# A linear-attention block and a gated MLP on one core: the second MLP product by Strassen's seven products, in items of 256 tokens by 1024 hidden columns

## The chip, the cores and the metric

The kernel runs on one core of a Trainium2 chip. The metric is device time in microseconds of one execution, the median of several. Engines are named as the profile names them: PE is the matrix engine (PEld its weight loads), DVE the vector engine, ACT the scalar engine with its function tables, POOL the general engine, SP the queue that issues most DMAs.

## The reference

Eight batches of eight heads, 576 tokens of width 64. Softmax of `q` over the head width, softmax of `k` over the tokens, then a linear attention, and a gated MLP over all 4608 tokens. `moe_w_in` and `moe_w_out` arrive as float64.

```python
q_s = softmax(q, axis=-1)            # per token
k_s = softmax(k, axis=2)             # per feature, over the tokens
kv  = einsum('bhsd,bhse->bhde', k_s, v)
x   = einsum('bhsd,bhde->bhse', q_s, kv)   # -> (4608, 512)
h   = x @ w_in                       # (4608, 512) @ (512, 2048)
sp  = maximum(h, 0) + log1p(exp(-abs(h)))
g   = h * erf(sp)
out = g @ w_out                      # (4608, 2048) @ (2048, 512)
```

## The kernel before, in words

**Precision.** An fp32 operand is written as the sum of two float16 tiles, a high and a low one (`split2`: ACT writes the high part, DVE the rest). A product of two such operands takes three float16 matmuls (high·high, high·low, low·high). A float32 matmul shows in the trace as two records. The first token block uses float32 matmuls in both MLP products, because the weights' split parts do not exist yet at that time.

**Weights.** Each of the eight jobs in `JOBS` is a quarter of `w_in` or `w_out`. A job is loaded as raw 64-bit words in two pieces (`wload`), turned into float32 by three DVE instructions for each piece (`wdecode`, `D` in the order), squared and reduced on ACT for a scale (`wsquares`, `Q`), and, once all eight are there, scaled in common (`wscales`, `Z`) and split (`wsplit`, `S`). For `w_in` the split also makes the sums that Strassen's scheme needs (`wsplit_sums`, `R`): seven operands in place of four. `w_out` is split plainly.

**First product.** It works in items: 384 tokens by 512 hidden columns, 12 blocks times 4 groups, 48 items, numbered n. `mm1(n, k)` (line 881 on) makes the seven Strassen products of an item, each of 12 matmuls of 192 columns into one of three PSUM banks X, Y and Z. The evacuations add them up in `H`: three by ACT, four by DVE. The operands of x, seven again, are made once per block by `finish`. Items 0 to 3 use `mm1_32`.

**Activation.** `softplus` and `erf` (`T`, `G`, line 337 in the trace, since both go through the helper `act`) run on ACT, each behind a load of its function table. `gmul` (`U`, line 984) multiplies on DVE. `ghi` and `glo` (`I`, `O`, lines 997 and 1001) split the result on DVE into two float16 halves, which lie in the memory of `H`.

**Second product.** `mm2(n, tt)` (line 1007 on) is plain: for each of three token tiles, four row blocks of `w_out` times three float16 matmuls of 512 columns (line 1029), accumulated over the four items of a block. Items 0 to 3 use float32 (line 1020). The last item's sum is scaled and moved out by one DVE instruction per token tile (line 1045), and SP issues the store.

**Attention.** `attention(b)` is a generator. Each `A` in the order, and `pace` later on, takes its next piece. It takes the two halves of the heads through column maxima of k, exponentials, the kv product and norms of q, then transposes q and makes x.

**What sets the order.** `ORDER` is a list by hand for items 0 to 3 and the weights. After it the loop over n emits, for each n, `U(n-1)`, the pieces of `m(n)`, of the split of n-1 and of `M(n-2)` interleaved, attention by `pace` against `SHARES`, and `T(n)`, `G(n)`. The framework then orders each engine's instructions by priority (order of emission) and by when its planner takes the operands to be there, so an engine's queue is not simply the order written. Each engine works its queue in order. A tile pool's `bufs` says how many copies of a tile exist, and a writer waits until the readers of the copy it takes are done.

```python
for n in range(4, N + 2):
    m0, m1, m2 = n < N, n - 1 < N, n - 2 < N
    if m1: tok(f"U{n - 1}")
    for i in range(4):
        if m0: tok(f"m{n}.{i}")
        if 4 < n <= N and i < 2: tok(f"{'IO'[i]}{n - 1}")
        ...
        if m2 and i < 3:
            tok(f"M{n - 2}.{i}")
            pace(n + (i + 1) / NTT)
```

## Time and profile before

| | us |
|---|---|
| median of three runs (lowest to highest) | 866.37 (865.97 to 866.99) |
| span of the profiled execution | 865.1 |
| PE busy, share of the span | 823.4, 95% |
| DVE busy | 642.5, 74% |
| ACT busy | 505.9, 58% |
| POOL busy | 18.2, 2% |

The page gives one time for the profiled execution, its span from the first to the last instruction. The median of the runs is 1.3 us above it, which is what lies around the span. Busy time is a union: where two instructions of an engine overlap, the time counts once. A "mean ns of one" is an instruction's own duration, and neighbours overlap by part of it. Matmuls overlap most: how often they follow each other is read from the start of one group to the start of the next.

### The profile page before, as it was taken

The numbers are of one execution on the slowest core, as the hardware profiler recorded it, in microseconds if no ns is written. First come the engines' busy times: TensorE is split into PE (matmuls) and PEld (weight loads), VectorE is DVE, ScalarE is ACT, GpSimd is POOL, SyncE is SP. The second block draws the span as 40 slices with busy tenths as digits, with TensorE's granted clock in tenths as the row PEclk, the third lists the DMA queues.
The fourth block names the chain that finished last, engine by engine and source line by source line (L and its number), as shares of the span: only waits on it lengthen the run. The fifth ranks groups of instructions, "written<-read, shape, count | busy, mean of one in ns | idle before, by whom it ended". The sixth has DMA issues, their size and how long they took to land.

```text
span 865.1 us, 15558 instructions
## 1 busy us (share of the span) xinstructions
PE 823.4 (95%) x6556; PEld 570.3 (66%) x6556; DVE 642.5 (74%) x923; ACT 505.9 (58%) x646; POOL 18.2 (2%) x37
## 2 busy tenths in 40 slices
PE   3999996889999999999999999999999999999997
PEld 2655555557766677767776677776776677677672
DVE  6999799899887778858866778867865656653543
ACT  2697677576584567466655467466655456453532
POOL 2101100000000000000000000000000000000000
PEclk9999998889999999999999999999999999999999
DMA  9976730041223202311141212311010000000100
GB/s 270 402 166 184 187 86 1 1 104 26 61 50 80 65 23 50 80 38 25 33 103 32 56 30 50 80 38 25 20 43 2 24 15 1 37 2 1 37 2 37
DMA packets 117381, 55.53 MB, mean 64 GB/s; under 512 B 106560, under 2 KB 108608, under 8 KB 117312
## 3 DMA queue, kind: packets, MB, share of 16 engines
q1 hardware_dynamic: 115136, 46.15, 20.3%
q0 software_dynamic: 2176, 8.39, 2.7%
q8 instruction: 51, 0.84, 0.4%
q14 instruction: 18, 0.15, 0.0%
HBM read 45.09 MB, written 9.44 MB: 63 GB/s over the span
## 4 chain that ended last, share of the span: by engine, by line
PE 73%; DVE 13%; ACT 6%; SPq 3%; DMA 2%; issue 2%; POOL 0%; ACTq 0%; DVEq 0%
PE o L1029 33%; PE pX L905 17%; PE pZ L905 8%; PE pY L905 4%; PE kv L535 3%; ACT L337 2%; ACT G L337 2%; SPq L402 2%; DVE wt L290 2%; PE o L1020 2%; DVE G L984 2%; PE x L625 2%; PE qT L610 1%; DVE H L1001 1%; DMA q<-in_q_dram 1%
## 5 line engine op out<-in xcount | busy, mean ns | idle before, releaser
L1029 PE MATMUL o<-wt,H 128*128 128x512 f16 x1584 | 366.9, 380 | 3.6 <-DVE H L997 3.1
L905 PEld LDWEIGHTS <-wt 128*128 128x128 f16 x3696 | 312.4, 99 | 37.5 <-issue 15.2
L1029 PEld LDWEIGHTS <-H 128*128 128x128 f16 x1584 | 152.4, 98 | 159.0 <-DVE H L997 4.1
L905 PE MATMUL pX<-x,wt 128*128 128x192 f16 x2112 | 208.0, 249 | 9.8 <-ACT H L924 5.7
L337 ACT ACT_TABLE_LOAD x105 | 134.7, 1283 | 7.9 <-DVE H L930 5.7
L984 DVE SCALAR_TENSOR_TENSOR G<-G,small,H 128x1536 f32<-128x1536 f32 x44 | 80.0, 1817 | 65.9 <-ACT G L337 65.8
L905 PE MATMUL pZ<-x,wt 128*128 128x192 f16 x1056 | 103.4, 247 | 0.0
L932 ACT COPY H<-pX 128x384 f32<-128x384 f32 x44 | 20.9, 476 | 139.7 <-PE pX L905 134.7
L337 ACT ACTIVATE G<-H,U 128x768 f32<-128x768 f32 (+1 forms) x60 | 72.8, 1231 | 22.1 <-DVE H L930 21.5
L1001 DVE TENSOR_TENSOR H<-G,H 128x1536 f16<-128x1536 f32 x44 | 77.3, 1756 | 1.1
L337 ACT ACTIVATE G<-G 128x1536 f32<-128x1536 f32 x48 | 71.2, 1484 | 0.5
L905 PE MATMUL pY<-x,wt 128*128 128x192 f16 x528 | 51.1, 246 | 0.5 <-DVE H L917 0.5
L436 ACT ACTIVATE x<-x 128x384 f32<-128x384 f32 (+1 forms) x52 | 17.6, 386 | 56.4 <-PE x L625 54.0
L917 DVE COPY H<-pY 128x384 f32<-128x384 f32 x44 | 24.4, 555 | 30.1 <-PE pY L905 30.1
L997 DVE CAST H<-G 128x1536 f16<-128x1536 f32 x44 | 42.0, 955 | 0.7
L290 DVE SCALAR_TENSOR_TENSOR x<-x,x 128x768 f16<-128x768 f32 (+1 forms) x44 | 37.2, 850 | 5.7 <-ACT x L289 5.6
L289 ACT ACTIVATE x<-x 128x768 f16<-128x768 f32 (+1 forms) x44 | 33.1, 762 | 12.2 <-DVE x L381 12.1
L1045 DVE TENSOR_SCALAR ob<-o,V 128x512 f32<-128x512 f32 x29 | 21.7, 749 | 23.9 <-PE o L1029 23.7
L930 DVE TENSOR_TENSOR H<-pZ,H 128x384 f32<-128x384 f32 x44 | 24.2, 551 | 19.3 <-PE pZ L905 19.3
L919 DVE TENSOR_TENSOR H<-pX,H 128x384 f32<-128x384 f32 x44 | 24.4, 555 | 15.3 <-PE pX L905 14.9
L535 PE MATMUL kv<-vbuf,k 128*64 128x65 f32 x480 | 22.0, 237 | 7.6 <-ACT k L337 5.2
L535 PEld LDWEIGHTS kv<-vbuf,k 128*64 128x64 f32 x480 | 18.7, 149 | 14.5 <-ACT k L337 6.4
(162 smaller groups left out, 823.1 us busy)
## 6 DMA issues: line engine op xcount, KB each, us to landing
out_dram<-ob SPq DMA_DIRECT2D x32, 256.0 KB, 2.2
vbuf<-in_v_dram SPq DMA_DIRECT2D x60, 128.0 KB, 3.0
q<-in_q_dram SPq DMA_DIRECT2D x56, 128.0 KB, 3.0
k<-in_k_dram SPq DMA_DIRECT2D x56, 128.0 KB, 3.3
wt<-in_moe_w_out_dram POOLq DMA_DIRECT2D x5, 1024.0 KB, 6.5
wt<-in_moe_w_in_dram SPq DMA_DIRECT2D x4, 1024.0 KB, 10.7
raw<-in_moe_w_in_dram SPq DMA_DIRECT2D x2, 1024.0 KB, 14.3
wt<-in_moe_w_out_dram SPq DMA_DIRECT2D x2, 1024.0 KB, 16.0
```

Of the source, the lines that this page charges most:

```text
L289: nc.scalar.activation(hi, src, AF.Copy, scale=s)
L290: nc.vector.scalar_tensor_tensor(lo, src, s, hi, op0=ALU.mult, op1=ALU.subtract)
L337: i = nc.scalar.activation(out_, in_, func, **kw)
L535: nc.tensor.matmul(bk[a * D:(a + 1) * D, c * W:(c + 1) * W], kk, vv, start=(t == 0), stop=(t == TM),)
L905: nc.tensor.matmul(o, w[wl][:, c, a * P:(a + 1) * P], x[:, xl, xi, c, :], start=(new and a == 0 and c == 0 and i == 0), stop=(c == 1 and i ...
L917: nc.vector.tensor_copy(C[0, 0], bank2("Y"))
L919: add(C[0, 0], bank2("X"), C[0, 0], op=ALU.add)
L930: add(C[0, 1], bank2("Z"), C[0, 1], op=ALU.add)
L984: nc.vector.scalar_tensor_tensor(flat(s["G"]), flat(s["G"]), GA[:, g:g + 1], flat(s["H"]), op0=ALU.mult, op1=ALU.mult,)
L997: nc.vector.tensor_copy(flat(s["gh"]), flat(s["G"]))
L1001: nc.vector.tensor_tensor(flat(s["gl"]), flat(s["G"]), flat(s["gh"]), op=ALU.subtract)
L1029: nc.tensor.matmul(o, s[gt][:, a, ts_], w[wl][:, a, :], start=(first_ and a == 0 and i == 0), stop=(last_ and a == FG - 1 and i == 2),)
```

## The change

The second product becomes a Strassen product too, and the items change shape: 256 tokens by 1024 hidden columns, 18 blocks times 2 groups, 36 items.

- `mm1` makes seven products of 24 matmuls with 128 columns, in two PSUM banks (X, Y), evacuated in tiles of 128x512: four by ACT, three by DVE.
- `mm2` makes seven products of 12 matmuls with 256 columns. The operands are made from G by `gsums` (four DVE instructions of 512 columns) and `gs` (four splits, three of 1024 columns and one of 512: the high part by ACT, the low part by DVE) into one buffer `GS`. `evacuate` adds up a block's output with seven DVE instructions of 256 columns and one on ACT (two more ACT scalings in blocks that hold tokens of two batches).
- The four `w_out` jobs are split into seven operands like those of `w_in`.
- Blocks 0 and 1 (items 0 to 3) do the second product in float32 (`mm2_32`); only block 0 (items 0 and 1) does the first one in float32 (`mm1_32`).
- The x operands are made in four parts (`finish` "a" to "d") inside the last item of the block before.
- Attention takes one half of the heads after the other, with one buffer for k instead of two (the second half's k and v are loaded after the first half's kv product), and is paced by `DUE`.
- In `ORDER` batch 1's attention stands behind the scales; all weights are decoded ahead of them.
- `H` has two buffers instead of three, `G` one instead of two, `ob` two instead of three.

```diff
-    ("in", 0), ("in", 1), ("out", 0), ("in", 2), ("out", 1), ("in", 3), ("out", 2),
-    ("out", 3),
-]
-CHAIN_FROM, CHAIN_TAIL = 2, 11
+JOBS = [(w, g) for w in ("in", "out") for g in range(4)]
+CHAIN_FROM, CHAIN_TAIL = 1, 6
...
-    m0.0 m0.1 D0.0.1 D0.1.1 D1.0 D1.1 m0.2 m0.3 T0 G0 Q0
-    D2.0 A m1.0 D2.1 m1.1 U0 m1.2 m1.3 T1 G1 Q1 A A D3.0 M0.0 D3.1 M0.1 M0.2 Q2 U1 A A
...
+    D0.0.1 D0.1.1 m0.0 m0.1 D1.0 D1.1 m0.2 m0.3 T0 G0 Q0 Q1
+    D2.0 D2.1 m1.0 m1.1 D3.0 D3.1 U0 m1.2 m1.3 Q2 Q3
+    D4.0 D4.1 D5.0 D5.1 T1 G1 M0.0 M0.1 Q4 Q5 D6.0 D6.1 U1 D7.0 D7.1 Q6 M1.0 Q7 M1.1
+    Z S0 R0 S1 R1 fa fb fc fd m2.0 m2.1 m2.2 m2.3 m2.4 m2.5 m2.6 T2 G2
+    A A S2 R2 A S3 R3 U2 A A A A A A A
+    m3.0 m3.1 fa m3.2 M2.0 m3.3 m3.4 fb fc M2.1 m3.5 fd m3.6 T3 G3 S4 R4 S5 R5
+    U3 M3.0 M3.1 S6 R6 S7 R7
...
+DUE = {2: 7, 3: 11, 4: 17, 5: 21, 6: 25, 7: 29}
+LEAD = 0.5
...
-        if which == "out":
-            split2(stg.pop(jn), whalf(jn, 0), whalf(jn, 1), s)
+        wsplit_n(jn, 0, sg[:, :, :256], 2)
+        wsplit_n(jn, 2, Q[1, 1], 1)
...
+        for o, x, y, op in sums:
+            nc.vector.tensor_tensor(Q[o], Q[x], Q[y], op=op)
...
+            t = at.tile(
+                [P, TM, 4, D], F32, tag=tag, bufs=1 if tag == "k" else 2, name=f"{tag}_{b}_{hf}"
+            )
...
+        if key == "a":
+            x_operands(i, "a", x[:, :, :P])
+            sub((0, 0), (0, 1), (0, 0))
+            sub((0, 1), (1, 1), (0, 1))
+        elif key == "b":
+            x_operands(i, "b", Bk[1, 1])
+            sub((1, 1), (1, 1), (0, 0))
+            sub((1, 0), (1, 0), (1, 1))
+        elif key == "c":
+            x_operands(i, "c", x[:, :, :P])
+        else:
+            x_operands(i, "d", x[:, :, P:])
+            x_next[0] += 1
...
         for hf in range(2):
+            ks = d["k"][hf]
...
+            kv_norm(b, hf, kv_mm(b, hf))
+            if hf == 0:
+                load_kv(b, 1)
+            elif b + 1 < B:
+                load_kv(b + 1, 0)
+            yield 1.5
+            q_norm(rows(qs[hf]), 16, f"q_{name}", b)
...
+    PRODS = [("Y", 1, 1), ("X", 0, 0), ("Y", 6, 3), ("X", 3, 6), ("Y", 4, 2), ("X", 5, 5),
+             ("X", 2, 4)]
...
+        for gi, jn in enumerate(jns):
+            w = [wop(jn, h, wi, 1)[:, 0] for h in range(2)]
+            for a in range(2):
+                o = s[b][:, (2 * gi + a) * P:(2 * gi + a + 1) * P]
+                for c in range(2):
+                    for t, (wl, xl) in enumerate(((0, 0), (0, 1), (1, 0))):
+                        nc.tensor.matmul(
+                            o, w[wl][:, c, a * P:(a + 1) * P], x[:, xl, c, :],
...
+        if k_ in (0, 2, 3, 6):
+            nc.scalar.copy(C[{0: (0, 0), 2: (1, 1), 3: (0, 1), 6: (1, 0)}[k_]], ev)
+        else:
+            o = C[{1: (0, 0), 4: (0, 1), 5: (1, 1)}[k_]]
+            add(o, ev, o, op=ALU.add)
...
-            for a in range(FG):
-                for i, (gt, wl) in enumerate((("gh", 0), ("gh", 1), ("gl", 0))):
-                    nc.tensor.matmul(
-                        o, s[gt][:, a, ts_], w[wl][:, a, :],
...
+    def gsplit(t, src):
+        nc.scalar.copy(t[:, 0], src)
+        nc.vector.tensor_tensor(t[:, 1], src, t[:, 0], op=ALU.subtract)
...
+        for o, x, y, op in ((
+            (S_[0], A[1, 0], A[1, 1], ALU.add), (S_[1], S_[0], A[0, 0], ALU.subtract),
+        ), (
+            (S_[2], A[0, 0], A[1, 0], ALU.subtract), (S_[3], A[0, 1], S_[1], ALU.subtract),
+        ))[e]:
+            nc.vector.tensor_tensor(o, x, y, op=op)
...
+        o = acc[bi][:, half * 256:half * 256 + 256]
...
+                for t, (gl, wl) in enumerate(((0, 0), (0, 1), (1, 0))):
+                    nc.tensor.matmul(
+                        o, g[:, gl, f, :], w[wl][:, a, :],
...
+        if k_ == 1:
+            nc.scalar.activation(ob[1][:, l], acc[0][:, l], AF.Copy, scale=1.0 if mixed else V[0])
+            plus(ob[0][:, l], 0, 1, ob[1][:, l])
+        elif k_ == 4:
+            plus(ob[1][:, l], 1, 1, ob[1][:, l])
+            plus(ob[0][:, r], 1, 0, ob[1][:, l])
+        elif k_ == 6:
+            plus(ob[1][:, r], 2, 0, ob[0][:, r])
+            plus(ob[0][:, r], 2, 1, ob[0][:, r])
+            plus(ob[1][:, l], 2, 0, ob[1][:, l])
+            plus(ob[1][:, l], 3, 0, ob[1][:, l])
...
+    def mm2_32(n, j):
...
+        for f in range(FT):
+            w = STG[JOBS.index(("out", 2 * u + f // 4))]
+            nc.tensor.matmul(
+                o, st[n]["H"][:, f, j * P:(j + 1) * P], w[:, f % 4, :],
...
+    FIN = {1: "fa", 4: "fb fc", 5: "fd"}
+    GSP = {0: "g{}.0", 1: "s{}.0 g{}.1", 2: "s{}.3", 4: "s{}.1", 6: "s{}.2"}
     for n in range(4, N + 2):
-        m0, m1, m2 = n < N, n - 1 < N, n - 2 < N
+        m0, m1, m2 = n < N, 4 <= n - 1 < N, 4 <= n - 2 < N
...
+        for i in range(7):
             if m0:
                 tok(f"m{n}.{i}")
...
+            if m2:
                 tok(f"M{n - 2}.{i}")
+            if m1:
+                for o in GSP.get(i, "").split():
+                    tok(o.format(n - 1))
+            if m0:
+                pace(n + (i + 1) / 7)
```

More of the change, by code (lines that the diff above doesn't have):

```diff
@@ L673, in attention @@
-        q_norm(rows(qs[1]), 16, f"q_{b}_1", b)
-        if j == 1:
+        yield 1.6
+        if tailq:
             q_norm(even["qt"], H, f"qt_{p}", b)
-        yield SHARES[8]
-        for i in ((3 * p + 1, 3 * p + 2) if j else (3 * p, 3 * p + 1)):
-            while not x_free(i):
-                yield 0
-        if j == 1:
+            yield 1.3
+        c0 = 0 if j == 0 else SM
+        blks = [x[0] for x in xcols(b, c0, SM if j == 0 else SM + P)]
+        while not all(x_free(i) for i in blks):
+            yield 0
@@ new lines, in vscale, with quad @@
+    def vscale(tau):
+        bs = batches(tau)
+        if len(bs) == 1:
+            return gscale(bs[0])
+        d = bat[bs[1]]
+        if "Vt" not in d:
+            d["Vt"] = at.tile([P, 1], F32, tag="Vt", bufs=1, name=f"Vt_{bs[1]}")
+            for a, b in enumerate(bs):
+                ps = slice(a * TAIL, (a + 1) * TAIL)
+                nc.vector.tensor_copy(d["Vt"][ps], gscale(b)[ps])
+        return d["Vt"]
+    def quad(t):
+        return t.rearrange("p (g q a) t -> p g q a t", g=2, q=2)
@@ L956, in unit @@
+    def unit(b, u):
+        U = bat[b]["U"][:, u:u + 1]
+        if b < 2 and (b, u) not in udone:
+            udone.add((b, u))
+            nc.vector.tensor_tensor(U, w_u["in"][:, u:u + 1], bat[b]["ux"], op=ALU.mult)
         return U
@@ L1046, in mm2, with evacuate, plus @@
-        if last_:
-            for dst, src in out_dmas(p, bk * NTT + tt, obs[i0, tt]):
-                nc.sync.dma_start(dst, src)
+                        o, g[:, gl, f, :], w[wl][:, a, :],
+                        start=(u == 0 and half == 0 and gi == a == t == 0),
+                        stop=(u == NU - 1 and gi == a == 1 and t == 2), skip_group_check=True,
+                    )
+        if u == NU - 1:
+            evacuate(i, k_)
+    def evacuate(i, k_):
+        V = [vscale(2 * i + j) for j in range(2)]
+        mixed = V[0] is not V[1]
+        if k_ == 0:
+            obs[i] = [at.tile([P, DM], F32, tag="ob", bufs=2, name=f"ob_{i}_{j}")
+                      for j in range(2)]
+        ob = obs[i]
+        l, r = slice(0, 256), slice(256, 512)
+        def plus(o, bi, half, y):
+            src = acc[bi][:, half * 256:half * 256 + 256]
+            if mixed:
+                nc.vector.tensor_tensor(o, src, y, op=ALU.add)
+            else:
+                nc.vector.scalar_tensor_tensor(o, src, V[0], y, op0=ALU.mult, op1=ALU.add)
+        if k_ == 1:
[9 more added lines that the diff above has]
+            plus(ob[1][:, l], 3, 0, ob[1][:, l])
+            for j in range(2):
+                if mixed:
+                    nc.scalar.activation(ob[j], ob[j], AF.Copy, scale=V[j])
+                out_dma(2 * i + j, ob[j])
@@ L1050, in attn_moe_kernel @@
     steps = start()
-    fn = dict(T=softplus, G=erf, U=gmul, I=ghi, O=glo)
+    fn = dict(T=softplus, G=erf, U=gmul)
     emitted_steps = set()
```

737 lines of the change are left out of this document (337 added, 400 removed).

## The prediction

> **What bounds the kernel now.** I read the page's busy shares, the busy time by stretches, then the chain in order of time for the length of a period, and the waits.
>
> ```profile
> PE 823.4 (95%) x6556; PEld 570.3 (66%) x6556; DVE 642.5 (74%) x923; ACT 505.9 (58%) x646; POOL 18.2 (2%) x37
> ```
>
> ```profile
> 0.00:22.00 22.00, 7.65 (x58) 5.87 (x59) 14.51 (x20) 6.03 (x6) 5.13 (x13) 1.00 1.04 273
> ...
> 800.00:865.00 65.00, 58.87 (x419) 36.88 (x416) 28.90 (x30) 25.89 (x25) 0.00 (x0) 1.00 0.07 25
> ```
>
> ```profile
> 22.00:200.00 178.00, 162.37 (x951) 102.48 (x950) 165.37 (x259) 130.52 (x198) 10.53 (x16) 0.94 0.47 137
> 107.00:200.00 93.00, 77.76 (x579) 54.98 (x578) 88.50 (x145) 65.83 (x83) 1.59 (x3) 0.89 0.18 45
> 254.00:450.00 196.00, 194.70 (x1738) 140.05 (x1737) 151.99 (x227) 113.72 (x140) 1.90 (x6) 1.00 0.22 54
> 420.50:435.20 14.70, 14.70 (x157) 11.23 (x156) 14.40 (x21) 10.01 (x13) 0.00 (x0) 1.00 0.29 80
> ```
>
> The columns are stretch, length, then busy PE, PEld, DVE, ACT, POOL, and the granted clock. There are two regimes. From 254 to 450 us PE works 194.70 of 196 us: PE is the bound, with DVE at 78% and ACT at 58%. From 107 to 200 us, where the weights are split, DVE is the bound: 88.50 of 93 us (95%), with PE at 84%. The first 22 us and the last 65 cost PE 14.4 and 6.1 us of idleness.
>
> ```profile
> 450.61 1.58 ACT G L337
> ...
> 646.31 1.58 ACT G L337
> ```
>
> ```profile
> DVE G L984 <- ACT G L337: 65.8, 33, 6.6
> ```
>
> The pattern of the chain repeats after 195.70 us, which is two batches: 12 items. DVE's longest wait is that of `U` for the error function: 65.8 us, 1.5 for each of the 44 items of line 984, 6.6 at most.
>
> **PE's part.** Start to start in the timeline gives what one matmul costs in a stream:
>
> ```profile
> 92.78 2.74 PE L944 MATMUL pZ<-x,wt 128*128 128x384 f32 x8
> 95.36 2.74 PE L944 MATMUL pX<-x,wt 128*128 128x384 f32 x8
> ...
> 104.21 2.74 PE L1020 MATMUL o<-sg,G 128*128 128x512 f32 x6
> 106.79 1.02 PE L622 MATMUL x<-qTs,kvbd 128*128 128x512 f32 x2
> ...
> 127.26 1.15 PE L905 MATMUL pY<-x,wt 128*128 128x192 f16 x12
> 128.25 1.15 PE L905 MATMUL pX<-x,wt 128*128 128x192 f16 x12
> ...
> 228.19 2.75 PE L1029 MATMUL o<-wt,H 128*128 128x512 f16 x12
> 230.78 1.15 PE L905 MATMUL pZ<-x,wt 128*128 128x192 f16 x12
> ```
>
> That is 82.5 ns at 192 columns (0.99/12), 215.8 at 512 (2.59/12), and 322 and 430 for a float32 record of 384 and 512. The line through the first two has 0.4166 ns a column; it gives 55.8 ns at 128 columns and 109.2 at 256, and 216 for a float32 record of 256 (twice the columns).
>
> No row has 128 columns. The nearest below is this one, of 64 columns, each with its own weight load:
>
> ```profile
> 277.63 0.83 PE L625 MATMUL xt<-qTt,kvbd 128*128 128x64 f16 x23
> 278.30 1.24 PE L1029 MATMUL o<-wt,H 128*128 128x512 f16 x5
> ```
>
> It gives 0.67/23 = 29 ns, on the same line (29.2). So weight loads don't hold a 128-column stream; I take 55.8, between 29 and 82.5 as bounds.
>
> An item before: 84 x 82.5 + 36 x 215.8 ns = 6.93 + 7.77 = 14.70 us. After: 168 x 55.8 + 84 x 109.2 = 9.37 + 9.17 = 18.55 us, for 4/3 of the work. Float32 records: before 4 x 16 x 2 = 128 in the first product and 4 x 12 x 2 = 96 in the second; after 2 x 32 x 2 = 128 and 4 x 16 x 2 = 128. Totals: before 44 x 14.70 + 128 x 0.322 + 96 x 0.430 = 729; after 34 x 9.37 + 32 x 9.17 + 128 x 0.216 + 128 x 0.430 = 695. PE is relieved of 34 us. A batch's attention costs PE (195.7 - 12 x 14.70)/2 = 9.65 us, unchanged.
>
> **DVE's part**, which the change loads:
>
> ```profile
> L984 DVE SCALAR_TENSOR_TENSOR G<-G,small,H 128x1536 f32<-128x1536 f32 x44 | 80.0, 1817 | 65.9 <-ACT G L337 65.8
> L1001 DVE TENSOR_TENSOR H<-G,H 128x1536 f16<-128x1536 f32 x44 | 77.3, 1756 | 1.1
> L997 DVE CAST H<-G 128x1536 f16<-128x1536 f32 x44 | 42.0, 955 | 0.7
> L919 DVE TENSOR_TENSOR H<-pX,H 128x384 f32<-128x384 f32 x44 | 24.4, 555 | 15.3 <-PE pX L905 14.9
> L604 DVE TENSOR_TENSOR qTs<-qT,qTs 128x512 f16<-128x512 f32 x24 | 16.5, 686 | 9.1 <-ACT qTs L603 9.1
> L290 DVE SCALAR_TENSOR_TENSOR wt<-wt,small,wt 128x1024 f16<-128x1024 f32 x12 | 15.1, 1280 | 2.3 <-ACT wt L289 2.3
> L315 DVE TENSOR_TENSOR wt<-wt 128x512 f32<-128x512 f32 x16 | 10.9, 684 | 0.0
> L491 DVE TENSOR_TENSOR kmax<-k 128x256 f32<-128x256 f32 x16 | 6.7, 418 | 0.1
> L290 DVE SCALAR_TENSOR_TENSOR wt<-wt,small,wt 128x2048 f16<-128x2048 f32 x2 | 4.7, 2348 | 0.0
> L290 DVE SCALAR_TENSOR_TENSOR wt<-wt,small,wt 128x512 f16<-128x512 f32 x4 | 3.0, 748 | 0.0
> ```
>
> Per item before: four evacuations of 0.555, 1.82, 0.955 and 1.756 = 6.7 us for 1536 columns. After, for 2048: three evacuations of 0.686, `U` 2.35, `gsums` 4 x 0.684, and splits of 3 x 1.22 (between the 512 and the 1536 row) and 0.686: 2.06 + 2.35 + 2.74 + 4.35 = 11.5 us. The cast goes to ACT, but it was DVE's cheapest. To this come, per item, 1.7 us of `evacuate` (seven times 0.48 per two items; 256 columns from the 512 and 1024 rows of line 290) and 2.2 us of `finish` (three 0.748, one 0.48, four 0.418 per two items): 15.4 us. Neighbours overlap by some 0.07 us each; 20 instructions make it 14.0.
>
> Over the kernel: evacuations 70, `U` 85, sums 88, splits 139, `evacuate` 54, `finish` 75 us against 390 before; the weights' splits 8 x 7.3 = 59 against 38; halved attention +4. That is +144, less 0.07 x 240 more instructions: +127, so 769 us of DVE. Attention stays near 27 us a batch: (152 - 12 x 6.25 - 9 x 0.68 - 3 x 5.0)/2 plus the halves.
>
> So in iterations 4 to 28, which carry six batches, PE needs 25 x 18.55 + 58 = 522 us and DVE 25 x 14.0 + 162 = 512. The cover under which DVE's extra work would be free is gone.
>
> **ACT.** Per item four copies of 0.59, `softplus` and `erf`, two table loads, and splits of 3 x 1.06 + 0.59 (`softplus` and `erf` are the 1536-column rows times 4/3, less their fixed part):
>
> ```profile
> L337 ACT ACT_TABLE_LOAD x105 | 134.7, 1283 | 7.9 <-DVE H L930 5.7
> L337 ACT ACTIVATE G<-H,U 128x1536 f32<-128x1536 f32 x28 | 44.1, 1576 | 0.3
> L337 ACT ACTIVATE G<-G 128x1536 f32<-128x1536 f32 x48 | 71.2, 1484 | 0.5
> L337 ACT ACTIVATE k<-k 128x1024 f32<-128x1024 f32 x14 | 14.7, 1056 | 10.6 <-DVE k L648 10.2
> L603 ACT CAST qTs<-qT 128x512 f16<-128x512 f32 x24 | 14.1, 588 | 19.1 <-PE qT L610 19.1
> ```
>
> That is 2.4 + 2.0 + 1.9 + 2.6 + 3.8 = 12.6 us, and some 16 with attention and `finish`, of 20.9: busy, not the bound, though it stands in the loop `erf`, `U`, splits, `M`. Table loads fall from 48 pairs to 36 and rise by one per batch.
>
> **The start.** The scales come at 111.4 us now, with batch 1's attention (some 26 us of DVE) ahead of them:
>
> ```profile
> 111.39 0.18 DVE L250 TENSOR_REDUCE small<-sq 128x8 f32<-128x32 f32 x1
> ```
>
> After, it stands behind them: scales at about 87. Then DVE owes 59 (splits) + 29 (batch 1) + 9 + 4 + 5 = 105, less overlaps 96 us; at the 95% of the stretch from 107 us, 101. Item 4 has its way from 188 us, with the first products of items 4 and 5 done by then in PE's gaps.
>
> **DMA queues.** The second half's k and v wait for the first half's kv product on SP, ahead of q loads and output stores:
>
> ```profile
> k<-in_k_dram SPq DMA_DIRECT2D x56, 128.0 KB, 3.3
> ```
>
> Four issues of about 1 us and 3.3 to land are some 7 us, twice per batch. I take 0: a batch has four items, 84 us. Uncovered, it would be up to 42 us for six batches. The single buffers of `G` and `GS` cost 0 as well: from one `softplus` to the next through `erf`, `U`, sums and two splits it is 6.5 + 7.0 = 13.5 us, under 18.55.
>
> **The sum.** From 188 us PE still has 32 x 9.17 + 30 x 9.37 + 6 x 9.65 = 632 us. The end costs about 9 (6.1 now, plus a longer way through `evacuate`). 188 + 632 + 9 = 829 if PE never waits. But DVE needs 512/25 = 20.5 us per item against PE's 20.87, and it now idles 1.5 us per item at `U`. I keep that wait, since nothing that causes it goes away: 22.0 us, 1.13 more than PE, 28 us over 25 items. Span 857; with 1.3 us around it, **858**. DVE would then be busy 93% in those iterations, as it is from 22 to 200 us (165.37 of 178).
>
> **The rivals.** *PE stays the bound:* the planner fills the 1.5 us with attention; 829 to 840, say 831 us. For it: the stretch from 420.5 to 435.2 us, one item long, with DVE 98% full and PE without a gap; against it: such stretches have slack on both sides, which 25 such items in a row have not. *DVE with a longer wait (slower):* in the loop of each item one ACT copy of a split (1.06 us) gets between the last evacuation and the error function, because ACT works in order and the copies are new there. DVE then idles 2.6 us per item: 2.2 more than PE, 56 us, 886 in all. The point from which it is no gain is 1.8 us of idleness per item ((865.1 - 829)/25 + 0.37), little above today's 1.5; that is why this rival weighs much. *Weight loads hold the short matmuls:* if a load couldn't hide behind a 128-column matmul, each would cost 99 ns, the length of a load:
>
> ```profile
> L905 PEld LDWEIGHTS <-wt 128*128 128x128 f16 x3696 | 312.4, 99 | 37.5 <-issue 15.2
> ```
>
> 5712 x 43 ns = 247 us more, over 1100. The 29 ns of the 64-column row speaks against it. The Trainium skill speaks for a milder form: "TensorE: Matmul & The Clock Gate", section "Back-to-back issue gap", gives about 81 ns per matmul in a stream at 128 columns with weight loads. By that figure 5712 x 25 ns = 144 us would be added, an estimate of about 1000 us. The same sentence has 131 ns at 512 columns, where this trace has 215.8, so I follow the trace.
>
> **How the numbers follow.** PE the bound: 0.14. The forecast: 0.46, its own range 845 to 868. The longer wait: 0.37. Weight loads: 0.03. A measurement of this kernel can tell 0.2% from no change, 864.6 to 868.1; the forecast's upper end and the rival's lower end each put 0.05 there. Faster 0.55, same 0.10, slower 0.35. The range goes from the first case's 832 to the third's 886.
>
> **What would show it.** Groups of 24 matmuls that start 1.34 us apart, and of 12 that start 1.31 apart, show PE's part. DVE near 769 us in all, above 90% from 22 us to the end of iteration 28, shows DVE's. The wait of `U` for the error function tells the first three cases apart: near zero, 1.5 or 2.6 us per item. The scales at 87 us and item 4's stream from 188 show the start. I am wrong if PE is idle under 2% in the middle, if its gaps are released by DMA, or if DVE's operations take other times than the rows.

## The result, and the profile after

The changed kernel takes 928.1 us (median of four runs, 925.1 to 930.5) against 866.4 us beside it: 1.070 times as long, interval 1.067 to 1.073. Forecast were 858 us; the range ended at 886. The profiled execution has a span of 925.6 us. The page's first line comes first, then the busy time by stretches (stretch, length, busy PE, PEld, DVE, ACT, POOL, granted clock):

```profile
PE 816.7 (88%) x9704; PEld 705.1 (76%) x9704; DVE 746.8 (81%) x1171; ACT 627.7 (68%) x810; POOL 17.3 (2%) x37
```

```profile
97.00:225.00 128.00, 99.57 (x1027) 74.28 (x1028) 113.30 (x182) 84.10 (x105) 3.17 (x6) 0.89 0.23 53
225.00:770.00 545.00, 504.67 (x6619) 456.05 (x6617) 449.03 (x724) 389.01 (x493) 2.52 (x8) 0.99 0.17 42
770.00:925.60 155.60, 137.09 (x1719) 125.26 (x1716) 97.94 (x137) 94.11 (x102) 0.00 (x0) 0.98 0.05 18
```

No engine is full in any stretch. In the middle, where the forecast had DVE at 93%, it is at 82% (449.03 of 545), and PE, which worked 194.70 of 196 us there before, at 93%. The cost of PE's work is as forecast; the timeline gives it from start to start:

```profile
848.68 1.50 PE L908 MATMUL pX<-xd,wt 128*128 128x128 f16 x24
850.02 2.78 PE L1041 MATMUL o<-wt,gs 128*128 128x256 f16 x24
852.64 1.00 PE L908 MATMUL pY<-xa,wt 128*128 128x128 f16 x15
```

That is 1.34/24 = 55.8 ns at 128 columns and 2.62/24 = 109.2 ns at 256. I took for every matmul of the trace the distance from the start before it, less the usual distance (the pitch) of its kind, as idleness: PE idles 50 us of 865 before and 143 us of 926 after. The rest of the span falls from 815 to 783 us; 13 us of it before and 15 after lie ahead of the first matmul and behind the last, so PE's own work falls by 34 us, as forecast. The whole loss is waiting. Of the 143 us, 63 lie ahead of 225 us, 63 from there to 770, 17 behind; before the change some 40, 10 and 2 us lay there, so most of what is new lies behind the start.

Where the kernel stands against the forecast is read from the starts of `U` (line 974), written U(n) for item n. These are U(4), U(28), U(34) and U(35):

```profile
215.55 2.34 DVE L974 SCALAR_TENSOR_TENSOR G<-G,small,H 128x2048 f32<-128x2048 f32 x1
...
759.91 2.35 DVE L974 SCALAR_TENSOR_TENSOR G<-G,small,H 128x2048 f32<-128x2048 f32 x1 [2.00 <-ACT G L307]
...
884.00 2.35 DVE L974 SCALAR_TENSOR_TENSOR G<-G,small,H 128x2048 f32<-128x2048 f32 x1 [2.53 <-ACT G L307]
...
903.69 2.35 DVE L974 SCALAR_TENSOR_TENSOR G<-G,small,H 128x2048 f32<-128x2048 f32 x1 [2.00 <-ACT G L307]
```

The forecast, worked back from its 857 us with some 18 from the last `U` to the end, 18.55 for each of the last seven items and 22.0 for the 24 before, has U(4) at 181. All runs in one table, in us (stages from the profiled execution):

| run | U(4) | items 5–28, each | items 29–35, each | to the end | median | ratio to before (interval) |
|---|---|---|---|---|---|---|
| forecast | 181 | 22.0 | 18.55 | 18 | 858 | 0.990 |
| changed kernel | 215.5 | 22.7 | 20.5 | 21.9 | 928.1 | 1.070 (1.067–1.073) |
| one table | 213.1 | 22.2 | 19.6 | 20.5 | 903.1 | 1.042 (1.040–1.044) |
| alternating banks | 216.1 | 22.2 | 20.3 | 21.9 | 914.9 | 1.057 (1.053–1.061) |
| block 1 in float16 | 215.5 | 22.8 | 20.5 | 21.6 | 930.3 | 1.073 (1.070–1.075) |
| plain second product | 213.9 | 22.3 | 19.7 | 19.2 | 907.9 | 1.047 (1.045–1.049) |
| q on POOL | 220.2 | 22.8 | 20.5 | 22.6 | 931.4 | 1.074 (1.071–1.077) |
| sums on POOL | 217.0 | 25.6 | 22.6 | 20.8 | 1010.4 | 1.163 (1.160–1.165) |
| attention pipelined | 216.3 | 22.5 | 20.5 | 21.6 | 925.4 | 1.066 (1.063–1.069) |
| four together | 218.7 | 24.6 | 21.6 | 20.8 | 980.8 | 1.130 (1.127–1.132) |
| no sums | 214.9 | 22.3 | 20.0 | 19.6 | 910.2 | 1.051 (1.048–1.054) |
| less PE | 216.0 | 21.6 | 19.2 | 19.7 | 890.2 | 1.027 (1.025–1.028) |
| item 4 first | 189.4 | 23.8 | 20.5 | 21.9 | 928.5 | 1.071 (1.069–1.072) |
| two GS buffers | 216.6 | 22.6 | 20.4 | 20.2 | 924.7 | 1.067 (1.065–1.068) |
| attention in even items | 222.3 | 22.5 | 20.5 | 21.9 | 929.5 | 1.071 (1.068–1.074) |
| attention in odd items | 208.6 | 22.9 | 20.5 | 23.1 | 927.0 | 1.069 (1.067–1.071) |
| U late | 217.3 | 22.7 | 20.8 | 23.1 | 929.0 | 1.071 (1.068–1.074) |
| even, banks, pipelined | 221.8 | 22.1 | 20.3 | 21.9 | 918.6 | 1.058 (1.055–1.061) |
| product 5 first | 206.8 | 22.9 | 20.8 | 20.3 | 922.8 | 1.065 (1.060–1.069) |
| the same, banks, pipelined | 210.1 | 22.6 | 20.8 | 21.9 | 922.0 | 1.063 (1.061–1.065) |

So the 69 us of span over the forecast are some 34 before U(4), 16 in the 24 items behind it, 14 in the last seven, where attention is over, and 4 at the end.

The last seven are the cleanest place to see why. These are the lines of one turn, from U(33) to U(34), that the reading below uses, in order of time; "..." marks rows left out:

```profile
864.41 2.35 DVE L974 SCALAR_TENSOR_TENSOR G<-G,small,H 128x2048 f32<-128x2048 f32 x1 [6.78 <-ACT G L307]
...
866.68 0.68 DVE L919 TENSOR_TENSOR H<-pX,H 128x512 f32<-128x512 f32 x1
...
867.42 1.50 PE L908 MATMUL pX<-xd,wt 128*128 128x128 f16 x24
...
871.43 0.68 DVE L919 TENSOR_TENSOR H<-pY,H 128x512 f32<-128x512 f32 x1
872.03 1.21 DVE L983 TENSOR_TENSOR gs<-H,gs 128x1024 f16<-128x1024 f32 x1
...
873.16 0.68 DVE L919 TENSOR_TENSOR H<-pX,H 128x512 f32<-128x512 f32 x1
873.89 1.50 PE L908 MATMUL pX<-xc,wt 128*128 128x128 f16 x24 [0.61 <-DVE H L919]
...
875.43 0.58 ACT L916 COPY H<-pX 128x512 f32<-128x512 f32 x1 [4.94 <-PE pX L908]
...
875.91 1.05 ACT L982 CAST gs<-H 128x1024 f16<-128x1024 f32 x1
...
876.98 1.28 ACT L307 ACT_TABLE_LOAD   x1
...
878.27 2.00 ACT L307 ACTIVATE G<-H,U 128x2048 f32<-128x2048 f32 x1
...
880.18 0.56 ACT L916 COPY H<-pY 128x512 f32<-128x512 f32 x1
...
880.77 1.28 ACT L307 ACT_TABLE_LOAD   x1
...
882.06 1.91 ACT L307 ACTIVATE G<-G 128x2048 f32<-128x2048 f32 x1
```

The busy time in its two parts, up to the end of the addition of product 5 (873.84) and behind it, in the same columns as above:

```profile
864.41:873.84 9.43, 8.35 (x119) 7.65 (x119) 9.43 (x11) 4.03 (x6) 0.00 (x0) 1.00 0.01 3
873.84:884.00 10.16, 10.11 (x144) 9.66 (x144) 1.92 (x2) 8.51 (x8) 0.00 (x0) 1.00 0.01 2
```

The next line is U(34) at 884.00, already shown. The products are counted from 0 to 6. DVE can't add product 1 (866.68) before U(33) is through, and product 3 waits for that bank (867.42). The sums, the splits and the addition of product 4 stand ahead of the addition of product 5 (873.16), and DVE works all 9.43 us up to its end. Product 6 goes into the same bank and waits for it (873.89). Then ACT copies it, puts in a split that stands in its queue (875.91), and only then comes softplus; a copy for the next item (880.18) stands ahead of the second table load. The turn takes 19.6 us, with PE's items of 18.55 inside it, though DVE is all but idle in the second part.

Over all items I split the period at the start of the addition of product 5, by the starts of lines 974 and 919. In the last seven it is 8.7 (even n) or 11.7 us (odd) from `U` to that addition, and 10.2 or 10.1 from it to the next `U`. In items 6 to 28 it is 10.0 and 13.7, then 10.7 and 11.8. Iterations alternate, 20.6 and 25.4 us, since `finish` and `evacuate` both fall into the odd ones. The turn shown is one of the even ones, which lose less.

The trace shows the same chain in the other turns. In the 30 turns from U(5) to U(35), DVE idles 0.05 us on average, and 0.5 at most, from `U` to the addition of product 5. Product 6 starts within 0.25 us of that addition's end in all but two turns. From its copy to the next `U`, ACT idles 0.12 us at most, and `U` starts 0.03 us behind the error function in 26 of the 30. So each period is a ring: first DVE's queue, then one product on PE, then ACT's queue, with hardly a gap.

### The profile page after: what moved, and what is told of

It is laid out like the page before. It is cut to its first block, busy times and chain, and to the rows that moved or that the text cites. A ratio compares the mean times of both kernels' runs of the same rounds, so it can differ in the third digit from the quotient of the medians.

```text
span 925.6 us, 22381 instructions
## 1 busy us (share of the span) xinstructions
PE 816.7 (88%) x9704; PEld 705.1 (76%) x9704; DVE 746.8 (81%) x1171; ACT 627.7 (68%) x810; POOL 17.3 (2%) x37
## 5 line engine op out<-in xcount | busy, mean ns | idle before, releaser
L1041 PE MATMUL o<-wt,gs 128*128 128x256 f16 x2688 | 333.4, 274 | 3.9 <-ACT gs L982 3.8
L1041 PEld LDWEIGHTS <-gs 128*128 128x128 f16 x2688 | 255.3, 98 | 42.3 <-issue 8.4
L974 DVE SCALAR_TENSOR_TENSOR G<-G,small,H 128x2048 f32<-128x2048 f32 x32 | 75.2, 2350 | 67.6 <-ACT G L307 67.6
L908 PE MATMUL pX<-xd,wt 128*128 128x128 f16 x1632 | 105.8, 221 | 6.6 <-DVE H L919 5.3
L983 DVE TENSOR_TENSOR gs<-H,gs 128x1024 f16<-128x1024 f32 x64 | 77.8, 1216 | 25.8 <-ACT gs L982 25.7
L982 ACT CAST gs<-H 128x1024 f16<-128x1024 f32 x64 | 66.8, 1043 | 32.1 <-PE o L1041 24.3
L307 ACT ACTIVATE G<-H,U 128x2048 f32<-128x2048 f32 (+3 forms) x46 | 71.0, 1556 | 0.4
L908 PE MATMUL pX<-xc,wt 128*128 128x128 f16 x816 | 53.2, 222 | 19.6 <-DVE H L919 19.4
L307 ACT ACTIVATE G<-G 128x2048 f32<-128x2048 f32 x36 | 68.8, 1911 | 0.4
L908 PE MATMUL pY<-xc,wt 128*128 128x128 f16 x816 | 54.2, 220 | 13.0 <-ACT H L916 7.3
L919 DVE TENSOR_TENSOR H<-pX,H 128x512 f32<-128x512 f32 x68 | 46.5, 684 | 23.6 <-ACT H L916 13.7
L908 PE MATMUL pY<-xa,wt 128*128 128x128 f16 x816 | 55.6, 225 | 3.6 <-DVE H L919 1.9
L916 ACT COPY H<-pY 128x512 f32<-128x512 f32 x68 | 39.4, 579 | 22.9 <-PE pY L908 17.2
L1088 PEld LDWEIGHTS o<-wt,H 128*128 128x128 f32 x96 | 18.7, 204 | 30.5 <-issue 19.4
```

What stands on the lines that cost most here:

```text
L307: i = nc.scalar.activation(out_, in_, func, **kw)
L908: nc.tensor.matmul(o, w[wl][:, c, a * P:(a + 1) * P], x[:, xl, c, :], start=(new and gi == a == c == t == 0), stop=(c == 1 and t == 2), sk ...
L916: nc.scalar.copy(C[{0: (0, 0), 2: (1, 1), 3: (0, 1), 6: (1, 0)}[k_]], ev)
L919: add(o, ev, o, op=ALU.add)
L974: nc.vector.scalar_tensor_tensor(h if n < 2 * NU else g, g, sc[:, u:u + 1], h, op0=ALU.mult, op1=ALU.mult)
L982: nc.scalar.copy(t[:, 0], src)
```

## The experiments

**Is it ACT's chain, or the sum of DVE's work?** One table for both functions:

```diff
-        act(g, g, AF.Erf, chain=in_chain(n))
+        act(g, g, AF.Softplus, chain=in_chain(n))
```

> The error function is replaced by a second softplus, so that ACT needs no table switch inside an item (the output is not the reference's); all else is as in the changed kernel (925.6 us of span, U(4) at 215.5 us, 22.7 us per item from item 4 to 28, 20.5 in the last seven). Theory 'loop' (U waits for softplus and erf, and DVE's next evacuation additions wait behind U and its splits): U comes 2.57 us earlier in each item, so that PE becomes the bound: 22.7 -> 20.9 us and 20.5 -> 18.6, 25 x 1.8 + 7 x 1.9 = 58 us less, about 868. Theory 'DVE throughput' (the sum of DVE's work sets the period): DVE's work is unchanged, 0 to 10 us less, 915 to 926.

Measured 903.1: 25 us less (21 between the two profiled executions), mostly from 0.46 us per item in the middle and 0.95 in the last seven, where 1.8 and 1.9 were expected. This is more than DVE's sum allows, and less than half of what the loop alone would give. From 225 to 750 us the wait of `U` for ACT fell from 41.5 to 14.6 us, but others rose: ACT's copies from bank X waited 57.7 us for PE instead of 45.6.

**Is it the banks?**

```diff
-    PRODS = [("Y", 1, 1), ("X", 0, 0), ("Y", 6, 3), ("X", 3, 6), ("Y", 4, 2), ("X", 5, 5),
+    PRODS = [("X", 0, 0), ("Y", 1, 1), ("X", 3, 6), ("Y", 6, 3), ("X", 5, 5), ("Y", 4, 2),
              ("X", 2, 4)]
...
+        if n % 2:
+            b = "Y" if b == "X" else "X"
...
```

> The seven products of the first product strictly alternate between banks X and Y, across items too, so that no product follows another one into its own bank (before: products 5 and 6 both into X, with an addition on DVE between). Work unchanged. Theory 'bank' (PE's waits come from a bank that is not yet evacuated): the 14 + 8 us of PE waits at pX<-xc and part of the 11 us at pY go, 20 to 25 us less, about 903. Theory 'loop': softplus still needs the addition of product 5, but product 6 and its copy (1.3 + 0.6 us) no longer stand behind it; up to 1.9 us per item where that addition is last: 10 to 40 us less. Theory 'DVE throughput': no change, 920 to 928.

914.9: 13 us less. From 225 to 750 us PE's waits at the two products that read `xc`, product 6 among them, fell from 19.8 to 8.6 us, but those at the two that read `xd` rose from 2.0 to 17.4. So part of the loss stands at the banks, and part of that only moved.

**Is it the float32 start?**

```diff
-    m3.0 m3.1 fa m3.2 M2.0 m3.3 m3.4 fb fc M2.1 m3.5 fd m3.6 T3 G3 S4 R4 S5 R5
-    U3 M3.0 M3.1 S6 R6 S7 R7
+    S4 R4 S5 R5 m3.0 m3.1 fa m3.2 S6 R6 m3.3 m3.4 fb fc S7 R7 m3.5 fd m3.6
+    g2.0 s2.0 g2.1 s2.3 s2.1 s2.2 T3 G3
...
```

> Block 1 (items 2 and 3) does its second product by Strassen in float16 as the later items do, with all of w_out split ahead of it, instead of in float32 with the split behind it. Theory 'start' (of the 68 us over the prediction some 33 are lost before item 4, because w_out is split in place only once the float32 products of items 2 and 3 have read it, and these wait for U(2) and U(3)): U(4) moves from 215.5 us to about 200, the total by -10 to -25 us, about 908; PE's own work falls by 27.5 - 18.3 = 9 us. Rival: the start is bound by DVE's sum of splits, attention and evacuations, which this edit raises by 2 x 7 us (sums and splits of G): no gain, 920 to 930.

930.3, no gain: U(3) comes at 189.9 instead of 172.8, U(4) at 215.5 as before. The rival's time came out. Its reason fits this run, in which DVE works 121.94 of the 128 us from 97 to 225, but not the plain second product below. Then item 4 ahead of the float32 block:

```diff
-    U3 M3.0 M3.1 S6 R6 S7 R7
+    U3 m4.0 m4.1 m4.2 m4.3 m4.4 m4.5 m4.6 T4 G4 M3.0 M3.1 S6 R6 S7 R7
```

> Order alone: the first product, softplus and error function of item 4 are emitted ahead of the float32 second product of item 3 and the last two splits of w_out. Theory 'order in the start' (before item 4, neither PE nor DVE is full: 99.6 and 113.3 of 128 us from 97 to 225; PE idles 6.8 us before that float32 block, and item 4's first product stands behind its 15 us): U(4) comes from 215.5 to about 197, PE's idleness falls by some 7 us and the total by 5 to 10, about 918. Rival: the total only follows when w_out is split, and that comes later by the time of item 4's products: no change or up to 5 more, 925 to 930.

928.5, no gain: U(4) comes 26 us earlier, but U(5) at 237.6 instead of 232.8, and nothing is left of it.

**What is Strassen's scheme worth in the second product?** The new items and first product, the second product plain:

```diff
+        if JOBS[jn][0] == "out":
+            split2(sg, whalf(jn, 0), whalf(jn, 1), wscale(jn))
...
+        for f in range(4):
+            for t, (gl, wl) in enumerate(((0, 0), (0, 1), (1, 0))):
+                nc.tensor.matmul(
+                    o, g[:, gl, f, j * P:(j + 1) * P], whalf(jn, wl)[:, f],
...
```

> Items stay 256 tokens by 1024 columns with the new first product, but the second product is plain again: G split once into two halves, w_out split once (no sums), 48 matmuls of 512 columns per item, one scaling per token tile. PE then needs 48 x 0.2158 = 10.36 us instead of 9.17 per item, +38 us over 32 items; DVE loses the sums (2.7), part of the splits (about 2) and the evacuation adds (1.7 less 0.7) per item, and some 20 us of splitting w_out in the start. Theories 'loop' and 'DVE throughput': the loop falls under PE's 9.37 + 10.36 + 2.3 = 22.0 us, so 25 x 0.7 + 7 x 0.8 us less there, and 15 to 20 less in the start: about 885. If instead PE's own sum set the period, it would be 925 + 38 - 15 = about 948.

907.9: with some 38 us more of PE's work (by the pitches) it is 20 us faster. In the last items PE is now full:

```profile
780.00:880.00 100.00, 100.00 (x1101) 71.45 (x1099) 45.83 (x53) 59.50 (x62) 0.00 (x0) 1.00 0.05 15
```

The gain expected in the start did not come: U(4) stands at 213.9. From 175 to 200 us DVE works 9.17 us in this run (the row below), in the changed kernel 21.80:

```profile
175.00:200.00 25.00, 23.17 (x182) 13.94 (x183) 9.17 (x14) 5.92 (x8) 0.00 (x0) 0.95 0.25 64
```

So the sum of DVE's work does not bound the start either. This run is still 41 us slower than the kernel before, with the second product plain in both: most of the change's loss is not the price of Strassen's scheme in the second product. Reckoned as above, PE idles some 22 us more than before up to 225 us, and some 16 more from there to 770.

**Can POOL take work from DVE?** First q's subtraction and scaling, then the sums of G:

```diff
-        nc.vector.tensor_tensor(
+        nc.gpsimd.tensor_tensor(
             t, t, m[:, :, None].to_broadcast([P, g, D]), op=ALU.subtract
...
```

> The subtraction and the scaling of q in attention (1.2 us each on DVE, five to six us a batch) go to POOL, which is nearly idle; POOL took 1.9 us for such a one in the start. Nothing in the item's own loop changes. Theory 'queue' (PE's waits in the middle, 61 us from 225 to 750, come from steps that stand behind other work in DVE's queue, which is 82% full there): DVE falls to about 77% there and PE's waits by a fifth to a third, total 12 to 20 less, about 912. Theory 'loop' (only U, sums, splits and evacuation additions count): 0 to 5 less, 921 to 928. If POOL and DVE hinder each other at memory, DVE's rows get longer and the total could rise.

```diff
-            nc.vector.tensor_tensor(o, x, y, op=op)
+            nc.gpsimd.tensor_tensor(o, x, y, op=op)
```

> The four sums of G per item (gsums, 4 x 0.68 = 2.7 us on DVE) go to POOL, at an estimated 1.0 us each (half of the 1.9 us row of 1024 columns). They stand inside the loop U -> sums -> splits, ahead of the splits of the sums. Theories 'queue' and 'loop' both: DVE is 2.7 us per item freer, the additions of products 4 and 5 stand behind less; the middle goes from 22.7 to about 21.5 us per item, the last seven from 20.5 to about 19: 25 x 1.2 + 7 x 1.5 = 40 less, about 887. Rival: the four sums are a chain (0 -> 1 -> 3), POOL is slower and the second and third split wait for it, H is held longer: no gain or worse, 925 or more.

931.4 and 1010.4: the first brings nothing, the second costs 82 us. The last section shows what lengthened; how much of the 82 us each part of it costs was not separated. The two with the banks and the pipelined attention:

> Alternating banks, q's two operations and the sums of G on POOL, and the pipelined attention together; the result stays the reference's. If the gains add up (13 measured for the banks, and 15, 40, 13 expected): about 845, below the kernel before (866). If they relieve one and the same wait, the best of them alone: about 885. Bound: PE's own work of 783 us plus the start's 63 us of PE idleness, which none of the four touches: 846.

980.8: slower than the changed kernel, as the sums on POOL alone were; how the four combine was not separated.

**Are attention's waits lost for good?**

```diff
-            bk = bank(f"x_{b}_{c}")
-            x_mm(b, c, bk, qT)
+            bk = bank(f"x_{b}_{c - 1}")
+            x_mm(b, c - 1, bk, qTs.pop(c - 1))
...
```

> Attention's four steps are pipelined by one: the transposes of q for column group c+1 are emitted ahead of the x product of group c, so that this product no longer follows at once on the copy (ACT) and the subtraction (DVE) that it needs. Work unchanged. Theory 'attention' (20 of the 61 us of PE's waits from 225 to 750 us stand at the x products, so they are lost there for good): these 20 fall to about 5 and the total by 12 to 15, about 912. Theory 'loop': PE is late elsewhere instead, the waits move to pX and pY and the total stays within 4 us, 922 to 928.

925.4, within the intervals of the changed kernel. PE's waits at the x products fell from 14.5 to 5.8 us as designed, but all its waits from 225 to 750 only from 61 to 57: most of them moved.

**What does a microsecond of each engine weigh?** Less work for DVE, then for PE:

```diff
-            nc.vector.tensor_tensor(o, x, y, op=op)
+            pass
...
-            src = flat(s["H"])[:, 1024 * (z - 1):1024 * z]
+            src = flat(s["G"])[:, 1024 * (z - 1):1024 * z]
```

> The four sums of G are left out and the second and third split read G instead (the output is not the reference's): DVE's own work falls by 2.7 us per item, PE's and ACT's stay. Theory 'DVE sets the period by its sum': the middle goes from 22.7 us to PE's 20.9 and the last seven from 20.5 to 18.6: 25 x 1.8 + 7 x 1.9 = 58 less, 867. Theory 'coupling' (two engines near full, bound to each other by in-order queues and single buffers, so that each waits for the other in turn): part of it, 21.8 and 19.5 us, 25 x 0.9 + 7 x 1 = 30 less, about 896.

```diff
-                for t, (gl, wl) in enumerate(((0, 0), (0, 1), (1, 0))):
+                for t, (gl, wl) in enumerate(((0, 0), (1, 0))):
```

> One of the three terms of each second product (high of G by low of w_out) is left out (the output is a little less exact): PE's work falls by 28 x 0.109 = 3.1 us per item, to 17.8 in the middle; DVE's and ACT's stay (DVE about 20.3 us per item in the middle). Theory 'DVE sets the period by its sum' and its wait for the error function: no change in the middle, 0 to 10 less in all, about 920. Theory 'coupling': PE's shorter queue brings the evacuations earlier; about a third of the 3.1 us, 25 x 1 + 7 x 1 = 32 less, about 894. Theory 'PE sets it': 25 x 1.8 + 7 x 2 and more, 865 or less.

910.2 and 890.2. DVE's 2.74 us per item bring 0.43 in the middle and 0.59 in the last seven; PE's 3.06 bring 1.08 and 1.33; ACT's 2.57 (one table) had brought 0.46 and 0.95. Per microsecond in the last seven that is 0.22 for DVE, 0.43 for PE and 0.37 for ACT; in the middle 0.16, 0.35 and 0.18. If the sum of one engine's work were the bound, the other two would bring nothing, and that one would bring 1 per microsecond if it is PE, or some 0.7 if it is DVE or ACT, because PE's own 18.55 and 20.9 us end the gain after 2.0 and 1.8 us. So no engine's sum sets the period. The last seven's three shares add up to 1.02, as the links of one closed chain would, but that proves nothing: the cuts are larger than what there was to gain, and the means hide opposite changes. Without the sums the odd turns of the last seven get 2.1 us shorter and the even ones 1.4 longer.

The two parts of the period, in the same last seven, show where a cut goes. With one table the second part loses 2.7 us (even) and 1.9 (odd), and the first gains 2.0 and 0.7. Without the sums the first loses 0.9 and 2.8, and the second gains 2.3 and 0.7. With less PE work DVE still has no gap in the first part, but in the odd turns fewer of its instructions stand there, 13 instead of 18, and this part takes 9.7 us instead of 11.7; why they are fewer was not shown.

**Is it the single buffer of GS?**

```diff
+    GS1 = cp.tile([P, 7 * 1024], F16, name="gs1")
...
-    def gop(z, n):
-        return GS[:, GO[z]:GO[z] + n * 1024].rearrange("p (h f t) -> p h f t", h=2, t=P)
+    def gop(z, n, it):
+        return (GS1 if it % 2 else GS)[:, GO[z]:GO[z] + n * 1024].rearrange("p (h f t) -> p h f t", h=2, t=P)
...
```

> Two buffers for the split operands of the second product (GS) instead of one; to have the memory, the low halves of w_out's quarters 1 to 3 lie in the same place as those of quarter 0 (the output is not the reference's; the work is). Theory 'single buffers': ACT's waits for PE at GS (24 us) and DVE's waits behind it (26 us) go, and the middle falls by about 1 us per item: 20 to 30 less, about 900. Theory 'loop through the error function': these waits only stand beside the loop; 0 to 6 less, 919 to 926.

924.7, 0.3% less, with overlapping intervals: not the cause. A second buffer of `G` and the third one of `H` were not run. The changed kernel's trace shows no wait that the first would end: before all of its instructions at line 307, softplus and the table loads among them, ACT idles 10.7 us, and none of it for an instruction that reads `G`. For one that reads `H` its copies wait once, 5.7 us. What other orders the planner would make with more buffers stays open.

**Is it the alternation?**

```diff
-        at_n += LEAD
+        pair, f = divmod(at_n, 2)
+        at_n = 2 * (pair + (0.8 * f if f < 1 else 0.8 + (1 - 0.8) * (f - 1))) + LEAD
```

> Order alone: attention's pieces are paced so that four fifths of them fall into the even iterations instead of half. In the changed kernel the iterations from U to U alternate: 20.6 us for even n with DVE busy 16.5, 25.4 us for odd n with DVE busy 22.0 (items 6 to 28), because the x operands (finish) and the output sums (evacuate) both fall into the odd ones. Theory 'alternation' (odd iterations are bound by DVE plus its wait for the error function, even ones by PE, and buffers one item deep can't even it out): with both near DVE 19.3 and PE 20.9 the pair goes from 46.0 to 43 or 44 us, 12 pairs, 24 to 36 less, about 897. Theory 'coupling' without it (every item loses about 2 us to waits, however DVE's work is spread): 0 to 6 less, 920 to 927.

> The opposite: one fifth of attention in the even iterations, four fifths in the odd ones. Theory 'alternation': odd iterations get some 4 us more of DVE work (26 us and the wait: 29), even ones stay at PE's time less the attention that went (about 18.6): the pair goes from 46.0 to 47.5 to 49 us, 18 to 36 more, about 952. Theory 'coupling': within 6 of the changed kernel.

929.5 and 927.0. The first did even out the iterations (22.0 and 23.6 us for even and odd n), the second drove them apart (19.8 and 26.0), and the sum stayed: the pair takes 45.6 and 45.8 us instead of 46.0, and U(4) moves as well, to 222.3 and 208.6. The theory falls.

**Does U stand in the way?**

```diff
-    GSP = {0: "g{}.0", 1: "s{}.0 g{}.1", 2: "s{}.3", 4: "s{}.1", 6: "s{}.2"}
+    GSP = {1: "g{}.0", 2: "s{}.0 g{}.1", 3: "s{}.3", 4: "s{}.1", 6: "s{}.2"}
...
-        if m1:
-            tok(f"U{n - 1}")
         for i in range(7):
+            if m1 and i == 1:
+                tok(f"U{n - 1}")
```

> Order alone: U of an item is emitted one seventh of an iteration later, behind the first product of the next item, and the sums and splits move back with it, so that DVE can put evacuations and attention into its wait for the error function (2.1 us per item). Theory 'loop' (DVE stands at U while products wait for their additions behind it): the wait falls to about 1 us, 1 us per item less, about 895. Rival: the wait is only filled with work that is ready anyway, and G and H come free later by as much: within 8 of 926, or slower.

929.0. Inconclusive: in the last items the addition of product 1 stands behind `U` in DVE's queue as before, so what was to be moved past it was not.

> Even pacing, alternating banks and the pipelined attention together. If the first brings 30 and the banks 13, they add up to about 880; if they relieve the same wait in odd iterations, about 895. Both leave it behind the kernel before (866).

918.6: no better than the banks alone (914.9).

**Does DVE's queue ahead of product 5's addition count?**

```diff
-    FIN = {1: "fa", 4: "fb fc", 5: "fd"}
-    GSP = {0: "g{}.0", 1: "s{}.0 g{}.1", 2: "s{}.3", 4: "s{}.1", 6: "s{}.2"}
+    FIN = {1: "fa", 5: "fb fc", 6: "fd"}
+    GSP = {0: "g{}.0", 1: "s{}.0 g{}.1", 2: "s{}.3", 5: "s{}.1", 6: "s{}.2"}
...
-                pace(n + (i + 1) / 7)
...
             tok(f"G{n}")
+            pace(n + 1)
```

> Order alone: the third split of G, three of the four parts of finish and all of attention's pieces are emitted behind the fifth product's addition (finish and the split right behind it, attention behind softplus and the error function). Theory 'ring' (the period is the time from U to the addition of product 5, 8.7 to 13.7 us of DVE's queue, plus a fixed 10 to 11.8 us from that addition through product 6, its copy, softplus, two table loads and the error function to the next U; DVE idles at the end of it): the first part falls by 2.5 us in the last odd items (11.7 -> 9.2) and by about 2 in the odd ones of the middle: 12 x 2 + 4 x 2.5 = 34 less; PE's 18.6 and 20.9 then come near, so about 900. Rival: work that waits behind the addition delays the release of G, GS and H or lies on PE's way in attention, and the second part grows by what the first loses: 920 or more.

922.8, 0.5% less, with overlapping intervals. In the odd iterations of the middle the first part falls from 13.7 to 11.9 us, but in the even ones it rises from 10.0 to 10.9; in the last odd ones 0.6 go and the second part gets 0.7 longer. There a split of 1.03 us now stands on ACT between softplus and the error function in all four turns, in the changed kernel in one of them:

```profile
854.85 2.00 ACT L307 ACTIVATE G<-H,U 128x2048 f32<-128x2048 f32 x1
856.76 0.71 ACT L1078 ACTIVATE ob<-ob,V 128x512 f32<-128x512 f32 x1
857.37 0.70 ACT L1078 ACTIVATE ob<-ob,Vt 128x512 f32<-128x512 f32 x1
857.98 1.03 ACT L982 CAST gs<-H 128x1024 f16<-128x1024 f32 x1
859.03 1.28 ACT L307 ACT_TABLE_LOAD   x1
```

> The same with alternating banks and pipelined attention: product 6 no longer waits for the addition of product 5 either, so the second part of the ring falls by up to 1.9 us where that addition is early. Theory 'ring': another 10 to 20 less than the run before, about 885. Rival: as there.

922.0, the rival's outcome again.

## Why the prediction was wrong

**Right.** PE's part: the pitches (55.8 and 109.2 ns), and with them the 34 us of relief. The weight loads do not hold a 128-column stream, which runs at these 55.8 ns; the 81 ns that the Trainium skill gives ("TensorE: Matmul & The Clock Gate", section "Back-to-back issue gap") do not occur here. The scales come at 83.7 us (forecast 87). DVE's new terms were sound: sums 86 us (forecast 88), splits 138 (139), `evacuate` 50 (54), and all its work 747 (769). ACT is no bound by the sum of its work (68% busy). The new k buffer costs little: DVE's largest wait for a DMA in the middle is 7.9 us in all, for q.

**Right by luck, the middle.** The forecast had 22.0 us per item in the middle, 20.5 of DVE's work and 1.5 of waiting, and 22.7 were measured. But DVE works 18.7 us per item there (449.03 us in 545 us, or 24 items) and idles 4.0. The term for its work was 1.8 us too large and the one for its waiting 2.5 too small, and the two nearly cancel. DVE "above 90% from 22 us" did not hold: it is 82% in the middle.

**Wrong, the start (34 us).** The step that failed is "item 4 has its way from 188 us, with the first products of items 4 and 5 done by then in PE's gaps". It took the start as the sum of DVE's work, with room on PE. The trace has, in PE's and DVE's queues:

```profile
172.78 2.34 DVE L974 SCALAR_TENSOR_TENSOR H<-G,small,H 128x2048 f32<-128x2048 f32 x1
...
175.17 5.40 PE L1088 MATMUL o<-wt,H 128*128 128x512 f32 x8 [6.77 <-DVE H L974]
180.41 3.60 PE L1088 MATMUL o<-gs,H 128*128 128x512 f32 x8
183.84 3.60 PE L1088 MATMUL o<-wt,H 128*128 128x512 f32 x8
187.27 3.60 PE L1088 MATMUL o<-gs,H 128*128 128x512 f32 x8
...
192.12 1.51 PE L908 MATMUL pX<-xd,wt 128*128 128x128 f16 x24
```

PE idles 6.77 us for U(3), does item 3's float32 block and only then, at 192, goes on with the first product of item 4. By 188 us three of its seven products were done and none of item 5's, where the forecast had both items' done. Neither PE (99.57) nor DVE (113.30) fills the 128 us from 97 to 225. Ahead of U(4) attention stands in ACT's queue: item 4's product 6 is copied at 199.85, but its softplus starts at 209.01, behind the exponentials of k and q (205.38 to 207.69). With the plain second product DVE works 95.3 us there instead of 113.3, and U(4) comes only 1.6 us earlier, so DVE's sum is not what holds the start. What would shorten it stays open: neither half precision for block 1 nor item 4 ahead of the float32 block did. The granted clock is another open share: from 97 to 150 us it was 0.81, where the kernel before had 0.94, and no run separates what that costs.

**Wrong, the single buffers at "cost 0", and with them the loop (30 us).** "From one softplus to the next through `erf`, `U`, sums and two splits it is 13.5 us, under 18.55" closed the wrong chain. The chain that exists goes from `U` through the sums, splits and additions queued behind it on DVE up to the addition of product 5, then product 6 on PE, then the copy, splits, table loads, softplus and error function on ACT to the next `U`: 19.6 us in the turn shown, 18.9 (even n) and 21.7 (odd) on average in the last seven, 20.6 and 25.4 in the middle. The prediction's 13.5 us hold `U`, the sums and two splits (7.0), softplus, the error function and their tables (6.5); they lack the additions and the third split in DVE's queue, product 6, and ACT's copies and split. The chain runs through the order of the queues rather than through the buffer that was tried: doubling GS brought 0.3%. The wait at `U`, kept at 1.5 us, was 2.1:

```profile
DVE G L974 <- ACT G L307: 67.6, 26, 6.8
```

That is 67.6 us over 32 items. For the last seven items no wait was forecast, and they take 2 us more than PE's 18.55 without any attention. What the prediction named as signs of being wrong (PE never idle, DMA, other durations) did not cover this.

**The rival that came nearest** is the slower one: an ACT split gets between the last evacuation and the error function. It is in the turn shown (875.91, 1.05 us). This rival had 0.37 of the chance and 886 us, 42 less than measured. It priced one copy; the chain had all of DVE's queue ahead of the addition on it, and the start was outside it.

**What stays open.** That the period is this ring is shown by the trace, turn by turn. It was not shown by breaking it: no order that was run brings the period down to PE's 18.6 and 20.9 us, and where a cut shortens one part, the other grows. Why the planner's order puts so much of DVE's work ahead of the addition, and what order would not, was not found. An order without ACT's splits and output scalings between the copy and the error function was not run. The start's loss is located but not explained.

## What to carry to other kernels

Fewer multiplications at the price of additions did not pay here, because the engine that adds stands on the chain: PE got 34 us less work and the kernel took 62 us more time, and the same kernel with a plain second product was 20 us faster. Before costing by the busy share of the fullest engine, follow one item round: from an instruction to its successor of the next item, through each engine's queue in its order, and compare that length with the bound. When no engine is full and a cut on any of them brings a fraction, suspect the order of the queues, and expect work that is moved within it to come back elsewhere, as it did in most of these runs.
